# A planner's transfer allowance, due times and slot table changed in a fused attention and gated-MLP kernel

## The chip, the cores and the metric

The program runs on one core of a Trainium2 chip. The metric is the device time of one execution in microseconds (us), lower is better; the number compared is the median of several executions. One execution was also profiled, and the rows below come from that one.

## What is computed

Two modules follow each other. The first is attention with heads mixed before and after the softmax; its output, turned to tokens by features, is the input of a gated block of three matrix products:

```python
# batch, n_heads, seq, head_dim = 4, 12, 448, 64
scores = scale * np.matmul(q, k.transpose(0, 1, 3, 2))
scores = np.einsum('bhij,hg->bgij', scores, w_pre)
scores = scores - np.max(scores, axis=-1, keepdims=True)
attn = np.exp(scores)
attn = attn / (np.sum(attn, axis=-1, keepdims=True) + 1e-09)
attn = np.einsum('bhij,hg->bgij', attn, w_post)
out = np.matmul(attn, v)
...
# n_tokens, d_model, d_ff = 1792, 768, 1536; x is out, heads side by side
gate = 1.0 / (1.0 + np.exp(-(x @ w_gate)))
val = x @ w_val
result = gate * val @ w_out
```

The weights arrive as 64-bit numbers and are cut to 32 bits on the chip. Matrix products of the gated block are done in float16, each float32 operand as a high and a low half (three matmuls instead of one), and blocks of two by two are multiplied with seven products instead of eight.

## The kernel before

**Attention** runs in slots, about 90 of them, each for one or two groups of ten query rows. A slot premixes (L216), takes the row maximum (L221, VectorE), the exponential (L228, ScalarE), scales (L240, GpSimd; L246, VectorE), mixes again (L258) and multiplies by v (L285). What else a slot does stands in a table, `plan`, that `at(slot, fn, ...)` fills. Among this is the preparation of the first eight of 36 weight pieces (`early`): four loads of a piece into one of three raw buffers, then `top` (ScalarE, GpSimd, ScalarE), `convert` and `peak_of` (VectorE) and a store of the float32 piece. A piece takes eleven steps, in eleven slots one after the other, and a new piece begins every eight slots from slot 10.

**The gated block** is a list of some 1,300 tasks that `order_tasks` puts in order before anything is issued. It walks through a clock of its own, gives each task a planned duration (`units`) on TensorE ("pe"), VectorE ("dve"), ScalarE ("act"), GpSimd ("pool"), the transfers that SyncE issues ("dma") or those that GpSimd issues ("keep"), and picks on each the open task with the earliest due time `late`. A task whose buffers are not free, or that would make its result too far ahead of `late` (table `AHEAD`), waits; `LEAVE` says how many buffers of a kind must stay free. The result is only an order: on the chip each engine works its list from the front, and a task whose input is missing holds up all that stand behind it on that engine. After a transfer the clock adds a fixed time before the result counts as there: 2.5 us, or 6.0 (`LATE`) in the part beside the attention.

There are six layers n (256 of the 1,536 hidden columns each) and two pairs p of batches. A layer and pair is seven products P1, P2, P6, P5, P7, P4, P3, each in two halves; a half is nine matmuls of 128x448 into one PSUM bank (`gate`, L1050). Between P1 and P6, and between P7 and P4, ScalarE copies the bank to a buffer of kind T (`copy`, L1070), since the next product is added onto it; sums (L1077) and the gate function (L1080, L1083) follow on VectorE and ScalarE, and the hidden values go to DRAM (`keep_h`, L1015). After all layers come the 21 steps of the output product for p = 0 and then for p = 1 (`out_mm`, L1061), each of three calls of six matmuls.

Every operand of a product is made by `round` (ScalarE, L1029: the high half) and `rest` (VectorE, L1034: the low half), after sums of blocks (`tt`, L1043). Both need a scale, and the scale needs the largest magnitude over all partitions. That is found by a chain: `peak` on VectorE (L924) reduces to one number per partition; `put_peak` (GpSimd, L927) stores 0.5 or 1 KB to DRAM; `get_peak` (SyncE, L930) loads it back spread over all partitions; `weigh` on VectorE (L934, then L910 to L913) gives the scale. The chain runs for layers 2 to 5 (`max_w`), once for w_out (`max_out`) and once for the hidden values of each pair (`max_h`). For w_out there are twelve pieces: raw load, conversion, store (`keep_w`, L999), load (`load_w`, L1002), 21 operands, their store (`keep_pair`, L1037) and, for each p, their load (`load_pair`, L1040). Stores of w_out's operands and the loads back are the transfers `w<-m` and `m<-w`.

## Time and profile before

| | us |
|---|---|
| median of three runs | 852.2 |
| the three runs | 855.54, 846.03, 852.2 |
| the profiled execution | 845.48 |
| its span, first to last instruction | 843.7 |

The profiled execution is 0.8% under the median of the three runs, and 1.78 us of it lie outside the span. Attention fills the first 362 us of the span, the layers stand up to 681 us, the output product for p = 0 up to about 768 and for p = 1 up to 840.

### The profile page before, as it was taken

What the parts mean: (1) busy time and instruction counts of PE and PEld (TensorE: products, weight loads), DVE (VectorE), ACT (ScalarE), POOL (GpSimd) and SP (SyncE); (2) the same over time, 40 slices, a digit from 0 to 9 for tenths busy, and PEclk for the clock granted to TensorE, in tenths of its full rate; (3) what the DMA queues carried; (4) which work ended last, traced back from release to release, by engine and by line L of the source; (5) the groups of instructions that cost most, each with busy time, mean ns of one, the idle gap of its engine ahead of it and who ended that gap; (6) DMA issues with size and microseconds to landing.
All of it is one profiled execution on the core that took longest, in us unless ns stands there. A gap on an engine that the chain in (4) does not pass through costs nothing.

```text
span 843.7 us, 23152 instructions
## 1 busy us (share of the span) xinstructions
PE 776.3 (92%) x9530; PEld 421.7 (50%) x9530; DVE 649.7 (77%) x1069; ACT 551.0 (65%) x1042; POOL 242.4 (29%) x422
## 2 busy tenths in 40 slices
PE   8899998999899998899799999999993997979998
PEld 2455554555455555554355455545551453535554
DVE  4998898889998997899887865799663898556500
ACT  3888887688688886886767655678653764253300
POOL 1544454344444443401122112222230222110000
PEclk9999999999999999999899999999996999989999
DMA  5786678857975756964244215557794798993001
GB/s 196 224 230 190 207 237 253 175 175 225 249 244 173 231 198 151 256 194 156 82 171 160 87 37 189 163 178 271 268 314 111 271 353 337 273 377 137 33 29 70
DMA packets 78689, 166.13 MB, mean 197 GB/s; under 512 B 20984, under 2 KB 54104, under 8 KB 78584
## 3 DMA queue, kind: packets, MB, share of 16 engines
q1 hardware_dynamic: 70920, 136.03, 52.7%
q0 software_dynamic: 7088, 28.13, 8.6%
q8 instruction: 74, 1.21, 0.6%
q10 hardware_dynamic: 576, 0.51, 0.2%
q14 instruction: 31, 0.25, 0.1%
HBM read 87.77 MB, written 38.15 MB: 149 GB/s over the span
## 4 chain that ended last, share of the span: by engine, by line
PE 49%; DMA 14%; DVE 11%; issue 11%; ACT 10%; POOL 3%; SPq 1%; ACTq 0%; POOLq 0%; DVEq 0%
PE bank L1050 17%; PE bank L1061 11%; PE av L285 6%; PE pm L216 5%; PE mx L258 5%; PE qk L158 4%; ACT e L228 4%; DVE m L1034 3%; DMA raws<-in_w_dram 3%; ACT mix L266 2%; DMA T<-st 2%; DVE nm L221 2%; DMA m<-xs 2%; DVE m L1043 1%; DMA m<-max_w 1%
## 5 line engine op out<-in xcount | busy, mean ns | idle before, releaser
L1050 PE MATMUL bank<-m,m 128*128 128x448 f16 x1116 | 217.1, 356 | 23.1 <-ACT m L1070 22.6
L1050 PEld LDWEIGHTS <-m 128*128 128x128 f16 x1512 | 148.6, 98 | 165.9 <-issue 30.4
L228 ACT ACTIVATE e<-pm,nm 128x448 f32<-128x448 f32 x180 | 115.1, 640 | 55.3 <-DVE nm L221 51.5
L240 POOL TENSOR_SCALAR ph<-e,ss 128x448 f16<-128x448 f32 x180 | 112.6, 638 | 62.1 <-DVE ss L234 41.1
L221 DVE TENSOR_REDUCE nm<-pm 128x1 f32<-128x448 f32 x180 | 103.3, 614 | 24.8 <-PE pm L216 23.8
L246 DVE SCALAR_TENSOR_TENSOR pl<-e,ss,ph 128x448 f16<-128x448 f32 x180 | 118.0, 695 | 0.8 <-POOL ph L240 0.8
L1061 PEld LDWEIGHTS <-m 128*128 128x128 f16 x756 | 75.0, 99 | 83.5 <-issue 16.8
L258 PEld LDWEIGHTS <-ph 64*128 64x128 f16 x2880 | 68.3, 94 | 79.0 <-issue 42.7
L266 ACT ACTIVATE mix<-mx 128x960 f32<-128x960 f32 (+1 forms) x92 | 102.8, 1117 | 2.7 <-PE mx L258 2.6
L216 PE MATMUL pm<-T,w 64*64 64x448 f32 (+1 forms) x720 | 99.1, 572 | 2.7 <-DMA T<-st 1.9
L158 PE MATMUL qk<-k,q 64*64 64x448 f32 (+2 forms) x640 | 94.4, 549 | 4.4 <-ACT st L164 4.0
L1061 PE MATMUL bank<-m,m 128*128 128x448 f16 x486 | 96.0, 352 | 0.0
L285 PE MATMUL av<-mix,v 128*64 128x120 f32 (+1 forms) x1504 | 94.0, 269 | 0.9 <-ACT xt L293 0.8
L258 PE MATMUL mx<-w2hi,ph 64*128 64x60 f16 x1440 | 71.9, 189 | 15.2 <-ACT mix L266 14.1
L285 PEld LDWEIGHTS av<-mix,v 128*64 128x64 f32 x1504 | 74.5, 139 | 8.2 <-issue 2.9
L1050 PE MATMUL bank<-m 128*128 128x448 f16 x396 | 77.4, 352 | 1.3 <-DVE m L1077 1.1
L233 POOL TENSOR_SCALAR ss<-ss 128x2 f32<-128x2 f32 (+1 forms) x92 | 35.6, 387 | 136.8 <-ACT e L228 136.0
L258 PE MATMUL mx<-w2lo,ph 64*128 64x60 f16 x1440 | 71.3, 188 | 3.0 <-issue 3.0
L258 PE MATMUL mx<-w2hi,pl 64*128 64x60 f16 x1440 | 71.2, 188 | 0.6 <-DVE pl L246 0.5
L258 PEld LDWEIGHTS <-pl 64*128 64x128 f16 x1440 | 62.0, 94 | 0.8 <-DVE pl L246 0.6
L1077 DVE TENSOR_TENSOR m<-bank,m 128x448 f32<-128x448 f32 x72 | 44.3, 618 | 22.3 <-ACT m L1070 10.8
L987 POOL CAST raws<-raws 128x768 f16<-128x768 bf16 x36 | 33.9, 943 | 93.8 <-ACT raws L984 93.8
(115 smaller groups left out, 1032.0 us busy)
## 6 DMA issues: line engine op xcount, KB each, us to landing
T<-st SPq DMA_DIRECT2D x176, 210.0 KB
m<-w SPq DMA_DIRECT2D x62, 384.0 KB
raws<-in_w_dram SPq DMA_DIRECT2D x28, 767.6 KB
hs<-m POOLq DMA_DIRECT2D x48, 224.0 KB, 2.6
m<-hs SPq DMA_DIRECT2D x15, 672.0 KB
w<-m POOLq DMA_DIRECT2D x21, 384.0 KB, 5.4
v<-in_vb_dram SPq DMA_DIRECT2D x12, 512.0 KB
raws<-in_w_dram SPq DMA_DIRECT2D x32, 191.9 KB
```

Source lines behind the costliest of these rows:

```text
L158: nc.tensor.matmul(sc[e][s0:s1, :S], lhsT=q[rows, c, s0:s1], rhs=k[rows, :], start=True, stop=True)
L216: nc.tensor.matmul(pm[bank][64 * x:64 * x + 64, :S], lhsT=w1[rows], rhs=T[rows, x], start=True, stop=True)
L221: nc.vector.tensor_reduce(nm[:, i:i + 1], pm[bank][:, :S], axis=AX.X, op=ALU.max, negate=True)
L228: nc.scalar.activation(out=e_t[u][:, i], in_=pm[units[u][2][i]][:, :S], func=AF.Exp, bias=nm_t[u][:, i:i + 1], scale=1.0, accum_out=ss_t[u ...
L240: nc.gpsimd.tensor_scalar(ph[:, i], e_t[u][:, i], ss_t[u][:, i:i + 1], 1.0, op0=ALU.mult, op1=ALU.mult)
L246: nc.vector.scalar_tensor_tensor(pl[:, i], e_t[u][:, i], ss_t[u][:, i:i + 1], p_t[u][0][:, i], op0=ALU.mult, op1=ALU.subtract)
L258: nc.tensor.matmul(mx[:, x, i, jb * HK:(jb + 1) * HK], lhsT=p[rows, i, JB[jb]:JB[jb] + 128], rhs=w[rows], start=(k == 0), stop=(k == 2))
L266: nc.scalar.activation(out=out.rearrange("p g (y r) -> p y g r", r=HALF), in_=mx_t.pop(u), func=AF.Copy, scale=1.0 / (P_UP * W_UP))
L285: nc.tensor.matmul(av_t[bi][64 * i:64 * i + 64, c % 4, :n], lhsT=vt[b, u][:, h + i, jb, :], rhs=mixes[bi % 2][:, jb, 2 * c + i, :n], start ...
L1050: self.nc.tensor.matmul(self.f32(bank), lhsT=w[a][:, k], rhs=x[b][:, k], start=self.START[i] and k == r == 0, stop=k == self.KH - 1 and r ...
L1061: self.nc.tensor.matmul(self.f32(bank), lhsT=w[a][:, k], rhs=b[bb], start=self.START[i] and j == k == r == 0, stop=j == OUT_TILES - 1 and ...
L1077: self.nc.vector.tensor_tensor(self.f32(out), self.f32(bank), self.f32(snap), op=ALU.add)
```

## The change

Seven things change. The names `w`, `wp`, `wq`, `q`, `T` are kinds of buffer or operand.

- Every planned transfer counts as landed 6.0 us after it (it was 2.5 in the gated block). The planned durations of a few tasks grow too.
- A table `DUE` moves the due times of groups of tasks: a group's tasks count as due so many us earlier (numbers below zero do nothing), and w_out's raw pieces and operands get due times of their own, from 120 and 127 us on the planner's clock.
- `AHEAD` and `LEAVE` get other numbers; the last region has seven buffers of kind T instead of five, and w_out's pieces may lie in buffers of kind B.
- The order of the first products: layer 1's P1 and P2 stand before layer 0's P6.
- The steps of an early raw piece stand in slots 0, 1, 2, 3 (the loads), then 8 to 12 and 14, a new piece begins every seven slots from slot 6.
- Small tiles that held top, up and down scales become parts of one tile.
- `sum_of` loops over the parts of its sum; there is one part, as before.

```diff
     for k in range(moe.EARLY):
-        for step in range(11):
-            at(10 + 8 * k + step, moe.early, k, step)
+        for step, slot in enumerate((0, 1, 2, 3, 0, 8, 9, 10, 11, 12, 14)):
+            at(6 + 7 * k + slot, moe.early, k, step)
         if k % 4 == 3:
-            for step in range(4):
-                at(20 + 8 * k + (0, 1, 3, 5)[step], moe.early_bound, k // 4, step)
+            for step, slot in enumerate((14, 15, 18, 21)):
+                at(6 + 7 * k + slot, moe.early_bound, k // 4, step)
...
-    LEAVE = dict(w=6, wp=1, wq=1, q=3, qp=1)
+    LEAVE = {'w': 7, 'wp': 3, 'wq': 12, 'q': 1, 'qp': 0}
...
-    ROOM = ((-15, dict(B=9, A=8)), (-7, dict(B=2, A=2, T=3)), (0, dict(B=3, A=5)), (9.6, dict(B=5, A=8, T=5, R=0)))
-    AHEAD = dict(raw=250.0, half=250.0, w=50.0, s=12.0, t=15.0, wp=15.0, wq=25.0, q=40.0, qp=15.0,
-                 c=40.0, snap=40.0, tmp=40.0, wide=40.0, hq=60.0, hqp=50.0, ow=120.0, os=120.0, owp=120.0)
+    DUE = {('raw', 2): -12.8, ('bound', 'w', 2): 72.0, ('w', 2): 20.3, ('raw', 3): -44.5, ('bound', 'w', 3): 106.5,
+        ('w', 3): -65.8, ('raw', 4): -107.6, ('bound', 'w', 4): 109.6, ('w', 4): -93.5, ('raw', 5): -334.4,
+        ('bound', 'w', 5): -183.5, ('w', 5): -156.2, ('w', 1): -149.8, ('x', 1): -35.5, ('bound', 'h', 0): -295.4,
+        ('h', 0): -462.6, ('bound', 'h', 1): 179.3, ('h', 1): -27.5, ('load_h', 0): 9.6, ('load_pair', 0): -8.7,
+        ('store', 0): -57.0, ('keep_h', 0): -7.8, ('sum_of', 0): 125.4, ('sigmoid', 0): 22.8, ('hidden', 0): -7.6,
+        ('copy', 0): -5.8, ('sum', 0): 54.2, ('load_x', 0): -59.0, 'raws': (120.6, 11.4), 'pairs': (127.3, 180.1)}
+    ROOM = ((-15, dict(B=9, A=8)), (-7, dict(B=2, A=2, T=3)), (0, dict(B=3, A=5)), (9.6, dict(B=5, A=8, T=7, R=0)))
...
+        steps = [(n, p, i) for n, p in order for i in range(NP)]
+        for at in (2, 3):
+            steps.insert(at, steps.pop(NP + at - 2))
+        for n, p, i in steps:
...
-            us = min(t.units.values()) + (2.5 if "dma" in t.units or "keep" in t.units else 0.1)
+            us = min(t.units.values()) + (self.LATE if "dma" in t.units or "keep" in t.units else 0.1)
...
+        for t in tasks:
+            t.late = min(t.late, self.soon(t))
...
-                end = now + us + ((2.5 if now >= 0 else self.LATE) if u in ("dma", "keep") else 0.1)
+                end = now + us + (self.LATE if u in ("dma", "keep") else 0.1)
...
+    def soon(self, t):
+
+        group = self.group(t)
+        if group[0] in ("raws", "pairs"):
+            first, step = self.DUE[group[0]]
+            lead = {self.load_raw: 15.0, self.top: 6.0, self.keep_w: -3.0, self.load_w: 15.0}.get(t.fn, 0.0)
+            return first + step * group[1] - lead
+        return t.late - self.DUE.get(group, 0.0)
```

Three places show what this does to the order. The first is **ScalarE in the layer stage p = 1, n = 4**, around the first work that needs the scale of p = 0's hidden values. Rows with `up_h0` (before) are operands that need this scale, rows with `one_out0` (after) need w_out's; COPY rows are the copies of a bank that free it for the next product. Before:

```order
L1070 COPY m_3_8615<-bank0_8447 128x448
L921 ACTIVATE junk_201,abs_h1_175<-m_3_8615 128x448
L1070 COPY m_3_8615<-bank1_8448 128x448
L1029 ACTIVATE m_0_7946<-m_3_8615,up_h0_167 128x1344
L1029 ACTIVATE m_2_8510<-m_2_8510,up_h0_167 128x1344
L1029 ACTIVATE m_3_8615<-m_0_7946,up_h0_167 128x1344
L1070 COPY m_1_8294<-bank0_8447 128x448
L1070 COPY m_1_8294<-bank1_8448 128x448
```

and the same place after the change:

```order
L1126 COPY m_1_8259<-bank0_8416 128x448
L1126 COPY m_3_8578<-bank1_8417 128x448
L1136 ACTIVATE m_3_8578<-m_3_8578,back1_166 128x448
L1085 ACTIVATE m_0_7912<-m_0_7912,one_out0_160 128x768
L1085 ACTIVATE m_3_8578<-m_2_8476,one_out0_160 128x768
L1085 ACTIVATE m_3_8578<-m_0_7912,one_out0_160 128x768
L976 ACTIVATE junk_167,abs_h1_159<-m_3_8578 128x448
L1126 COPY m_1_8259<-bank0_8416 128x448
L1126 COPY m_3_8578<-bank1_8417 128x448
```

Three operands of w_out stand there now, where three of the hidden values stood; the first operand with h0's scale comes 24 rows later.

The second place is **VectorE at the end of the layer stage p = 0, n = 5 and the beginning of the next**, between w_out's `peak` and its `weigh` (the reduction into top_out0, or one_out0, from an m tile). The L1077 rows (after: L1133) are sums of a bank of TensorE. Before:

```order
L924 TENSOR_REDUCE top_out0_176<-abs_out0_180 128x1
L1043 TENSOR_TENSOR m_1_8294<-m_1_8294,m_0_7946 128x1344
L1034 SCALAR_TENSOR_TENSOR m_0_7946<-m_3_8615,up_h0_167,m_0_7946 128x1344
L1034 SCALAR_TENSOR_TENSOR m_2_8510<-m_2_8510,up_h0_167 128x1344
L1077 TENSOR_TENSOR m_3_8615<-bank2_8449,m_1_8294 128x448
L1077 TENSOR_TENSOR m_3_8615<-bank3_8450,m_1_8294 128x448
L1034 SCALAR_TENSOR_TENSOR m_3_8615<-m_0_7946,up_h0_167,m_3_8615 128x1344
L934 TENSOR_REDUCE top_out0_176<-m_1_8294 128x1
```

and after:

```order
L980 TENSOR_REDUCE one_out0_160<-abs_out0_162 128x1
L1133 TENSOR_TENSOR m_3_8578<-bank6_8583,m_1_8259 128x448
L1133 TENSOR_TENSOR m_3_8578<-bank7_8584,m_3_8578 128x448
L1139 SCALAR_TENSOR_TENSOR m_3_8578<-m_3_8578,back0_165 128x448
L1139 SCALAR_TENSOR_TENSOR m_3_8578<-bank5_8582,back0_165,m_3_8578 128x448
L1133 TENSOR_TENSOR m_3_8578<-bank6_8583,m_1_8259 128x448
L1133 TENSOR_TENSOR m_1_8259<-bank7_8584,m_3_8578 128x448
L1139 SCALAR_TENSOR_TENSOR m_3_8578<-m_1_8259,back0_165,m_3_8578 128x448
L980 TENSOR_REDUCE one_h0_154<-abs_h0_156 128x1
L1133 TENSOR_TENSOR m_3_8578<-bank2_8418,m_1_8259 128x448
L990 TENSOR_REDUCE one_out0_160<-m_3_8578 128x1
```

w_out's chain now begins first, and h0's `peak` stands inside it. Between the two ends of w_out's chain the sums run from P7 on bank 6 over P3 on banks 6 and 7 to the next stage's P2 on bank 2, eight halves of products; before they ran over two sums of one product.

The third place is **SyncE's list in the output product of p = 0**, around the load of the second pair's largest hidden value. L1040 (after: L1096) loads an operand of w_out, L1019 (L1075) a block of hidden values. Before:

```order
L1040 DMA m_2_8510<-w16_132 128x1536
L1019 DMA m_3_8615<-hs_133 128x1344
L1019 DMA raws_63<-hs_133 128x1344
L1040 DMA m_3_8615<-w16_132 128x1536 x3
L930 DMA m_3_8615<-max_h1_174 128x128
L1040 DMA m_2_8510<-w16_132 128x1536
```

and after:

```order
L1096 DMA m_0_7912<-w16_132 128x1536
L1096 DMA m_3_8578<-w16_132 128x1536
L1096 DMA m_2_8476<-w16_132 128x1536
L986 DMA m_3_8578<-max_h1_158 128x128
L1075 DMA m_2_8476<-hs_133 128x1344
L1096 DMA m_0_7912<-w16_132 128x1536 x3
```

The load of max_h1 stood behind 21 of the 42 loads of w_out's operands and behind all blocks of hidden values; now it stands behind 8 of them and ahead of the second pair's blocks.

## Rows read from the trace of the kernel before

**Rows 1.** The page, part 1: busy us, share of the span, instructions.

```profile
PE 776.3 (92%) x9530; PEld 421.7 (50%) x9530; DVE 649.7 (77%) x1069; ACT 551.0 (65%) x1042; POOL 242.4 (29%) x422
```

**Rows 2.** TensorE's timeline: start, us, line, count, [idle before <- who ended it].

```profile
406.32 10.08 PE L1050 MATMUL bank<-m,m 128*128 128x448 f16 x45 [7.06 <-ACT m L1070]
...
485.91 44.43 PE L1050 MATMUL bank<-m,m 128*128 128x448 f16 x234
...
648.23 8.59 PE L1050 MATMUL bank<-m,m 128*128 128x448 f16 x36 [14.67 <-ACT m L1070]
656.66 6.97 PE L1050 MATMUL bank<-m 128*128 128x448 f16 x36
...
713.61 4.93 PE L1061 MATMUL bank<-m 128*128 128x448 f16 x18 [4.92 <-DMA m<-w]
...
745.23 6.17 PE L1061 MATMUL bank<-m 128*128 128x448 f16 x18 [6.26 <-ACT m L1068]
```

**Rows 3.** ScalarE's timeline around 612 to 662 us.

```profile
643.74 4.03 ACT L1029 ACTIVATE m<-m,up_h 128x1344 f16<-128x1344 f32 x3 [13.08 <-DVE up_h L913]
647.67 0.94 ACT L1070 COPY m<-bank 128x448 f32<-128x448 f32 x2
```

**Rows 4.** VectorE's timeline, same stretch.

```profile
622.47 0.17 DVE L924 TENSOR_REDUCE top_h<-abs_h 128x1 f32<-128x24 f32 x1
...
642.66 0.29 DVE L934 TENSOR_REDUCE top_h<-m 128x1 f32<-128x128 f32 x1 [11.42 <-DMA m<-max_h]
...
643.62 0.15 DVE L924 TENSOR_REDUCE top_out<-abs_out 128x1 f32<-128x12 f32 x1
...
656.74 0.29 DVE L934 TENSOR_REDUCE top_out<-m 128x1 f32<-128x128 f32 x1 [5.81 <-DMA m<-max_out]
```

**Rows 5.** VectorE's and ScalarE's timelines around 715 to 750 us.

```profile
727.00 0.17 DVE L924 TENSOR_REDUCE top_h<-abs_h 128x1 f32<-128x24 f32 x1
...
742.16 0.29 DVE L934 TENSOR_REDUCE top_h<-m 128x1 f32<-128x128 f32 x1 [10.53 <-DMA m<-max_h]
...
743.25 1.42 ACT L1029 ACTIVATE m<-m,up_h 128x1344 f16<-128x1344 f32 x1 [18.56 <-DVE up_h L913]
```

**Rows 6.** VectorE's timeline around 430 to 450 us.

```profile
435.29 0.15 DVE L924 TENSOR_REDUCE top_w<-abs_w 128x2 f32<-128x8 f32 x1
...
444.91 0.42 DVE L934 TENSOR_REDUCE top_w<-m 128x2 f32<-128x256 f32 x1 [2.59 <-DMA m<-max_w]
```

**Rows 7.** Tile view of max_h, then of max_w: time to landing of the stores.

```profile
DMA to landing us min/median/max: 8.0/10.7/13.4
...
DMA to landing us min/median/max: 3.2/3.2/3.7
```

**Rows 8.** Busy time by stretch: TensorE, its weight loads, VectorE, ScalarE, GpSimd, clock, DMA.

```profile
380.00:400.00 20.00, 19.21 (x101) 9.76 (x100) 20.00 (x28) 14.19 (x24) 3.34 (x2) 1.00 0.42 158
500.00:520.00 20.00, 20.00 (x108) 10.32 (x107) 10.92 (x14) 10.23 (x20) 3.27 (x5) 1.00 0.46 156
660.00:680.00 20.00, 19.53 (x104) 9.90 (x102) 20.00 (x25) 17.05 (x29) 5.40 (x10) 1.00 0.93 315
```

**Rows 9.** Transfers by line: count, KB each, median us to landing.

```profile
w<-m POOLq DMA_DIRECT2D x21, 384.0 KB, 5.4
```

**Rows 10.** What SyncE waited for, 600 to 745 us: total, times, longest.

```profile
SPq L1040 <- DMA w<-m: 62.7, 19, 10.2
```

**Rows 11.** Waits in the attention, 30 to 360 us: ScalarE, then TensorE.

```profile
ACT raws L984 <- DMA raws<-in_w_dram: 5.1, 2, 2.8
...
PE pm L216 <- DMA T<-st: 1.9, 3, 0.9
```

**Rows 12.** The chain that ended last, its transfers of 40 to 260 us.

```profile
62.67 5.10 DMA raws<-in_w_dram
...
128.90 7.20 DMA raws<-in_w_dram
...
220.96 8.22 DMA T<-st
```

More of the change, by code (lines that the diff above doesn't have):

```diff
@@ L512, in __init__ @@
         for g, (e, c) in list(groups.items()) + [(("x", p), (1, 0)) for p in pairs]:
-            for kind in ("top", "up", "down"):
-                self.one[(kind,) + g] = top.tile([128, e], F32, name="%s_%s%d" % ((kind,) + g))
+            one = top.tile([128, 3 * e], F32, name="one_%s%d" % g)
+            for i, kind in enumerate(("top", "up", "down")):
+                self.one[(kind,) + g] = one[:, i * e:(i + 1) * e]
             if c:
@@ L518, in __init__ @@
         for p in pairs:
+            back = top.tile([128, 2 * self.FN + 1], F32, name=f"back{p}")
             for n in range(self.FN + 1):
-                self.one["back", p, n] = top.tile([128, 2 if n < self.FN else 1], F32, name=f"back{p}_{n}")
+                self.one["back", p, n] = back[:, 2 * n:min(2 * n + 2, 2 * self.FN + 1)]
         self.junk = top.tile([128, 512], F16, name="junk")
@@ L583, in split @@
         uses = ((by, False),) if known else ()
-        more = 0.15 if by[1] == "w" else 0.0
+        more = 0.25 if by[1] == "w" else 0.07
         self.task(self.round, dict(act=self.by_act(n)["act"] + more), ((f, False), (pair, True)) + uses, pair, f, by)
@@ L745, in gathered @@
         if i in (P1, P6, P7):
-            task(self.copy, self.by_act(S), [(a, False), (("snap", p, n, i, e), True)] + more, ("snap", p, n, i, e), a, back)
+            task(self.copy, dict(act=0.53 if n < self.FN else 0.63), [(a, False), (("snap", p, n, i, e), True)] + more, ("snap", p, n, i, e), a, back)
         if i in (P2, P7, P3):
@@ L816, in order_tasks @@
                     need = self.place(t, free)
-                    if t.late + lag - now > 40.0 and any(free.get(self.KIND[name[0]], 0) < dict(raw=2).get(name[0], 0)
+                    if t.late + lag - now > 40.0 and any(free.get(self.kind(name), 0) < dict(raw=2).get(name[0], 0)
                                                          for name in t.new if name[0] in self.KIND):
@@ L855, in order_tasks, with group, tile_of, kind @@
                 self.users[name] = self.users.get(name, 0) + 1
+    def soon(self, t):
[5 more added lines that the diff above has]
+        return t.late - self.DUE.get(group, 0.0)
+    def group(self, t):
+        N, a = 4 * self.FN, t.args
+        if t.fn in (self.load_raw, self.top, self.convert, self.keep_w, self.peak_of):
+            k = a[{self.load_raw: 0, self.top: 0, self.peak_of: 2}.get(t.fn, 1)]
+            if t.fn == self.peak_of:
+                k += N if a[1][0] == "out" else 4 * a[1][1]
+            return ("raws", k - N) if k >= N else ("raw", k // 4)
+        if t.fn in (self.peak, self.put_peak, self.get_peak, self.weigh):
+            return ("raws", 4 * OUT_TILES) if a[0][0] == "out" else ("bound",) + a[0]
+        if t.fn in (self.load_w, self.round, self.rest, self.tt, self.keep_pair):
+            name = a[1] if t.fn in (self.round, self.rest) else a[0]
+            if t.fn == self.keep_pair:
+                return "pairs", a[1]
+            if name[0] in ("w", "s", "wp"):
+                n = self.order[name[2]][0] if name[0] == "w" else name[2]
+                return ("pairs", n - self.FN) if n >= self.FN else ("w", n)
+            return ("h", name[1][0]) if type(name[1]) is tuple else ("x", name[1])
+        return t.fn.__name__, 0
+    def tile_of(self, name):
+        if name[0] == "w" and name[2] >= 4 * self.FN:
+            return self.order[name[2]][0] - self.FN
+        if name[0] in ("s", "wp") and name[2] >= self.FN:
+            return name[2] - self.FN
+        return -1
+    def kind(self, name):
+        return "B" if name[0] in ("w", "s") and self.tile_of(name) >= 0 else self.KIND.get(name[0])
     def ahead(self, name):
@@ L896, in f32 @@
             return self.banks[name[1]][:, :self.S]
-        return self.at[name][:, :self.WE] if name[0] == "raw" else self.at[name]
+        return self.at[name][:, :self.WE] if name[0] in ("raw", "w", "s") else self.at[name]
     def f16(self, name):
@@ L920, in sum_of @@
     def sum_of(self, h, g, c):
[L921 removed]
+        h, e = self.f32(h), self.abs[g].shape[2]
+        n = h.shape[1] // e
+        for i in range(e):
+            self.nc.scalar.activation(out=self.junk[:, :n], in_=h[:, i * n:(i + 1) * n], func=AF.Abs,
+                                      accum_out=self.abs[g][:, c, i:i + 1])
     def peak(self, g):
```

48 lines of the change are left out of this document (24 added, 24 removed).

## The prediction, made before the changed kernel was run

> **What bounds the kernel now.** The page's first part says that TensorE is busy for 776.3 of the 843.7 us of the span [rows 1]; so only its idle time can be won, and the next view is TensorE's timeline after the attention, read for the brackets that give idle time and who ended it. Four idle times stand out [rows 2]. The chain of waits, followed back from each, names the cause.
>
> A: 14.67 us before 648.23. It ended with ScalarE's copy of a bank, which stood behind three operands that needed h0's scale; those had waited 13.08 us [rows 3]. The scale was late since the chain peak, store, load, weigh took from 622.47 to 642.66, 20.2 us; VectorE had reached `weigh` 11.42 us before the answer came [rows 4].
> B: 7.06 us before 406.32, between layer 0 and layer 1, again on a copy [rows 2].
> C: 4.92 us before 713.61, on a load of an operand of w_out (m<-w) in p = 0's output product [rows 2].
> D: 6.26 us before 745.23. h1's chain took from 727.00 to 742.16, 15.2 us; VectorE waited 10.53 of them, ScalarE 18.56 [rows 2, 5].
>
> After an idle time TensorE starts slowly. After A 36 matmuls took 8.59 us where the next 36 took 6.97: 1.6 more. 234 in a row took 44.43, so 0.190 each; by that 45 are 8.55 and 18 are 3.42 us, and the restarts after B, C and D cost 1.5, 1.5 and 2.75 [rows 2]. So A is worth 16.3, B 8.6, C 6.4 and D 9.0 us, 40.3 in all. Nearly all else after the attention is matmuls that must be done.
>
> **A and the longer allowance.** The planner let 2.5 us pass after each transfer; a chain of store and load was thus planned far too short. In the task list before, four to six halves of products stand between `peak` and `weigh` of every chain; after the change eight for w_out, nine for h0, eight or nine for layers 2 to 5, and fourteen calls for h1. A half is nine matmuls, 1.71 us; a call of the output product six, 1.14 us. That gives w_out's chain 13.7 us of covered time, h0's 15.4 and h1's 16.0. Measured lengths of the chain are 9.6 us for a layer [rows 6], 13.1 for w_out's (643.62 to 656.74), 20.2 for h0's [rows 4] and 15.2 for h1's [rows 5]. By its own length w_out's wait is nil and h0's 4.8; by the shortest nil, by the longest 6.5 for w_out. An idle us of VectorE cost TensorE 14.67 / 11.42 = 1.3. h0's length was taken while GpSimd's small store queued among w_out's raw pieces; in SyncE's new list eleven transfers stand between the last of these and h0's load (it was three). I therefore take 2 of A's 16.3 us as left: gain 14.3, bounds 16.3 and 7.9 (6.5 x 1.3 left). What hides the longer wait is the sums and the operands of the earlier products that VectorE and ScalarE do meanwhile; in the place of h0's three operands before the two copies stand three of w_out's, which hang on the other chain. If that is late, the same copies are late again.
>
> One rule speaks against the six us. The row says that the landing of a store of half a KB took 8.0 to 13.4 us for h and 3.2 to 3.7 for the layers [rows 7]. The Trainium skill, page "DMA: Bandwidth & Descriptors", section "Anatomy of one DMA — SWDGE (gpsimd) path", gives such a store a fixed 2.0 us or so and size over bandwidth on top; by it 2.5 us would do, A and D would owe nothing to the allowance, and the sum below would hold 12.0 in place of 34.8 us. The trace disagrees, by 1.2 us in calm stretches and by 11 in full ones.
>
> **D, by the due time of h1's bound.** It moves from behind 21 loads of operands to behind 8. Covered time 16.0 us against its own 15.2: nothing is left; against 20.2, 4.2 x 1.3 = 5.5. I take 0.5 left: gain 8.5, bounds 9.0 and 3.5. Late next there is VectorE itself: it is busy for all of 20 us at 660 to 680 [rows 8].
>
> **C, operands of w_out.** The load that was missing is that of the ninth step (P6, last third). Before, its operand's store stands eight calls ahead of its use (9.1 us) and the load five; the trace made this 9.1 + 4.92 = 14.0 us. Now fourteen calls lie between store and use, 16.0 us, so it fits by 2. In SyncE's list the load is eleventh among its kind, not fourteenth, but h1's load now stands ahead of it, and behind SyncE's wait for h1's store are queued all loads of operands and blocks: at the longest landing of 13.4 us [rows 7] that is 7.4 more than planned. The store of an operand lands in 5.4 us as a median [rows 9], and SyncE waited 62.7 us for these in 19 waits, 10.2 the longest [rows 10]; 10.2 would make 14.0 into 18.8, 2.8 us of idle time and a slow start. Bounds: 6.4 gained, or 0.5 lost (7.4 less the 2 that fit is 5.4, and the start's 1.5, against 6.4 now). I take 5.
>
> **B, the swapped products and more T buffers.** Layer 1's P1 and P2, four halves or 6.8 us, now stand ahead of layer 0's P6, on inputs that layer 0's P1 and P2 have already used; two more T buffers let the copies go. That covers most of B, if the operands are there. Against it: at 380 to 400 VectorE is busy for 20.00 of 20 us [rows 8], so that it, not the order, may set the pace, and layer 1's operands must now be made before others. Bounds 8.6 gained, 3.4 (one product) lost; I take a little under half of what B is worth, 4.
>
> **w_out's pieces, the layers' chains.** Twelve raw loads, conversions and stores move to earlier layers, beside TensorE work that hides them; five of w_out's raw pieces now stand ahead of the layers' last eight. That costs nothing while the chains of layers 3 and 5 have fourteen halves from `peak` to first use, 23.9 us, against 9.6 [rows 6] or at worst 20.2 [rows 4]. Tiles joined, the loop in `sum_of`, the longer planned durations: no instruction is added, nothing.
>
> **Attention.** ScalarE waited 5.1 us in two waits for raw pieces [rows 11], and the chain that ended last goes through raw loads of 5.10 and 7.20 us [rows 12]. Five slots instead of two between the last load and its use remove these. But a piece every seven slots puts loads at other slots, in front of other loads of T, and one of these of 8.22 us is on the chain too [rows 12]. Bounds 5.1 gained, 8.2 lost; since TensorE waited for T for 1.9 us in all [rows 11], I take 3 gained.
>
> **Sum.** 14.3 + 8.5 + 5 + 4 + 3 = 34.8 us. The span goes from 843.7 to 808.9; with 1.8 us outside it the profiled execution from 845.5 to 810.7. The median stands at 852.2 / 845.48 = 1.008 times the profiled one, so 817. A measurement of this kernel can tell a difference from none from about 1% on.
>
> **Rivals.**
> Traffic decides. A landing is not a constant: it grows with what is under way, 3.2 to 13.4 us in one trace [rows 7], and six us only fits the calm stretches. Every chain beside the output product then takes h0's 20.2 us: A gains 7.9, D 3.5, C 2.1 (2.8 and a 1.5 restart stay), B 4, the attention nothing: 17.5, a profiled execution of 828, a median of 835. The Trainium skill has the rule in the same page, section "Queues, rings and completion order": a semaphore's increment lands only after every earlier write of its DMA engine, across its queues. The three lengths of one chain agree with it. Against it speaks that w_out's raw pieces are out of the way.
>
> VectorE becomes the bound. At 660 to 680 it has no gap [rows 8]; if what C and D lose in waits returns as operands that come just too late, A, B and the attention remain, 21.3: 824, a median of 831. Against it: in the middle of the layers it is busy for only 10.92 of 20 us [rows 8], and the earlier pieces go there.
>
> It doesn't do what it says. The list does show the wider chains; but if the idle time only moves (to layers 3 and 5, whose `weigh` now stands six halves before the first use instead of about twenty), within 1% of now: 848.
>
> Slower: the early raw pieces block the regrouping of the scores. SyncE's list is worked from the front, eight pieces bring 32 loads into other slots, and each T behind them holds up a slot. If each piece costs one T wait of 8.22 us where three raw waits cost about 17.5 on the chain now (two of them in [rows 12], the third about as long as the first), that is 65.8 - 17.5 = 48 us in the attention against 31.8 won after it: 862 profiled, a median of 869. It decides from (31.8 + 8.5 + 17.5) / 8, some 7 us per piece on. Against it: the 1.9 us that TensorE waited for T [rows 11].
>
> **How the numbers follow.** The forecast with its own scatter (806 to 826) has 0.56, traffic 0.18, VectorE 0.12, no change 0.07, slower 0.07. The likeliest is the forecast: 817. All gains at their best (16.3 + 9.0 + 6.4 + 8.6 + 5.1 = 45.4) give 807 as a median, and the runs before lie 0.7% below theirs: low end 804. The high end takes in most of the traffic rival: 838. Faster by over 1% (under 843.7) are the forecast, traffic and VectorE: 0.86; the same 0.08; slower 0.06.
>
> **What would show it.** In the profile after: the three `weigh` rows of h0, w_out and h1 with little idle time before them; no TensorE idle time over 3 us in the layers' second half; SyncE's load of h1 soon after the output product begins; ScalarE without waits for raw pieces in the attention. Wrong would be: idle before `weigh` as long as now, an m<-w wait on TensorE again, slots of the attention over 6 us more often than now, or VectorE busy without a gap while TensorE waits.

## The result

The changed kernel takes 822.6 us (median of four executions, 821.23 to 825.83) against 852.2 (846.03 to 855.54): a ratio of 0.9666, 95% interval 0.9603 to 0.9729. The forecast was 817, with a range of 804 to 838.

The profiled executions differ by less, 845.48 to 825.83, since the one of before is 6.7 us under its median and the one of after 3.2 above: 19.7 + 6.7 + 3.2 = 29.6. So the stages below add up to the smaller difference. In the spans (843.7 and 824.1) the three stages moved thus: the first `gate` product begins at 362.63 before and 370.85 after, 8.2 us lost; from there to the first product of w_out 318.7 and 305.4, 13.3 won; the output product 162.4 and 147.9, 14.5 won.

The page of the changed kernel, part 1, answers to [rows 1]; TensorE has the same number of matmuls.

```profile
PE 773.0 (94%) x9530; PEld 420.4 (51%) x9530; DVE 650.3 (79%) x1069; ACT 554.0 (67%) x1042; POOL 243.6 (30%) x422
```

TensorE's timeline after the change answers to [rows 2]. L1106 is `gate`, L1117 `out_mm`, L1085 and L1090 make operands, L1133 is a sum of two banks.

```profile
384.64 0.55 PE L1106 MATMUL bank<-m,m 128*128 128x448 f16 x2 [2.91 <-ACT m L1085]
...
386.64 13.67 PE L1106 MATMUL bank<-m,m 128*128 128x448 f16 x62 [1.45 <-DVE m L1090]
...
638.06 3.52 PE L1106 MATMUL bank<-m,m 128*128 128x448 f16 x9 [6.19 <-DVE m L1133]
641.38 3.99 PE L1106 MATMUL bank<-m 128*128 128x448 f16 x18
...
704.41 7.55 PE L1117 MATMUL bank<-m,m 128*128 128x448 f16 x39 [0.78 <-DMA m<-w]
```

The bracket of D (6.26) is gone, C is 0.78 for 4.92, B 2.91 and 1.45 for 7.06. B still has a slow start: 62 matmuls at 0.190 are 11.8 us and took 13.67, so 6.3 of B's 8.6 us remain. A is still there with 6.19 and a slow start: 9 matmuls at 0.190 are 1.71 and 18 are 3.42 us, so 3.52 and 3.99 hold another 2.4. Of A's 16.3 us 8.6 remain.

Who holds A is seen in VectorE's timeline, the answer to [rows 4, 5]: `peak` (L980) and `weigh` (L990) of w_out, of h0, of h1.

```profile
611.13 0.17 DVE L980 TENSOR_REDUCE one_out<-abs_out 128x1 f32<-128x12 f32 x1
...
622.14 0.18 DVE L980 TENSOR_REDUCE one_h<-abs_h 128x1 f32<-128x24 f32 x1 [0.74 <-ACT junk L976]
...
636.39 0.29 DVE L990 TENSOR_REDUCE one_out<-m 128x1 f32<-128x128 f32 x1 [10.60 <-DMA m<-max_out]
...
646.56 0.28 DVE L990 TENSOR_REDUCE one_h<-m 128x1 f32<-128x128 f32 x1
...
680.44 0.17 DVE L980 TENSOR_REDUCE one_h<-abs_h 128x1 f32<-128x24 f32 x1
...
699.13 0.29 DVE L990 TENSOR_REDUCE one_h<-m 128x1 f32<-128x128 f32 x1 [2.33 <-DMA m<-max_h]
```

It is w_out's chain now: 25.3 us from `peak` to `weigh`, where it was 13.1, and VectorE waits 10.60 us for it. Both of its transfers are long. The store goes out at 611.59, the load can follow at 624.94, and its data are there at 636.39 (timelines of GpSimd and of SyncE's queue):

```profile
611.59 0.54 POOL L983 DMA_DIRECT2D max_out<-one_out  x1 [0.35 <-DVE one_out L980]
...
624.94 0.32 SPq L986 DMA_DIRECT2D m<-max_out  x1
```

h0's chain takes 24.4 and h1's 18.7, but with nine halves and fourteen calls ahead of their `weigh` VectorE waits for h0's not at all and for h1's 2.33 us. ScalarE's operand behind w_out's scale waits 10.98, and the sum that TensorE waits for at 638 stands behind `weigh` on VectorE. The tile views of max_h, max_out and max_w, for [rows 7], say how long the stores of the peaks took to land:

```profile
DMA to landing us min/median/max: 11.8/12.6/13.5
...
DMA to landing us min/median/max: 13.3/13.3/13.3
...
DMA to landing us min/median/max: 3.5/4.7/6.3
```

So the layers' stores of 1 KB landed after 4.7 us as a median, and the half KB of h's and w_out's, near the output product, after 11.8 to 13.5. The busy time by stretch, for [rows 8], shows that VectorE is not what holds A: at 620 to 640 it works for 5.47 of 20 us. At 380 to 400, where B was, it still has no gap.

```profile
380.00:400.00 20.00, 15.50 (x74) 7.15 (x72) 20.00 (x26) 13.86 (x23) 0.00 (x0) 0.91 0.80 269
...
620.00:640.00 20.00, 13.81 (x69) 6.86 (x68) 5.47 (x13) 4.81 (x9) 1.62 (x3) 0.88 0.77 144
...
660.00:680.00 20.00, 20.00 (x107) 10.33 (x106) 18.75 (x23) 17.61 (x27) 4.02 (x8) 1.00 0.85 301
```

In the attention, TensorE's waits and the chain that ended last (the first of its loads; all are counted from 0 to 365 us) answer to [rows 11, 12]. ScalarE no longer waits for raw pieces, as forecast; but loads of T are on the chain seven times with 50.7 us, where it was three times with 18.3, and TensorE's own wait for T is 4.7 for 1.9.

```profile
PE pm L216 <- DMA T<-st: 4.7, 6, 2.4
```

```profile
106.81 2.79 DMA T<-st
...
133.75 8.59 DMA T<-st
...
153.62 10.88 DMA T<-st
...
165.95 5.09 DMA raws<-in_w_dram
...
191.53 8.55 DMA T<-st
```

Three questions follow. What of the 28 us after the attention comes from the six us, and what from the order? Did the new slots cost the 8.2 us in the attention? Why do the chains take 24 us, and can A's rest be had?

### The profile page after: what moved, and what is told of

Its sections match the earlier page's. It is cut to its first block, busy times and chain, and to the rows that moved or that the text cites. A ratio compares the mean times of both kernels' runs of the same rounds, so it can differ in the third digit from the quotient of the medians.

```text
span 824.1 us, 23147 instructions
## 1 busy us (share of the span) xinstructions
PE 773.0 (94%) x9530; PEld 420.4 (51%) x9530; DVE 650.3 (79%) x1069; ACT 554.0 (67%) x1042; POOL 243.6 (30%) x422
## 4 chain that ended last, share of the span: by engine, by line
PE 61%; DMA 14%; ACT 10%; DVE 9%; issue 5%; POOL 1%; SPq 0%; ACTq 0%; DVEq 0%; POOLq 0%
PE bank L1106 27%; PE bank L1117 14%; DMA T<-st 6%; PE av L285 6%; PE pm L216 6%; PE mx L258 4%; PE qk L158 4%; ACT e L228 4%; DVE nm L221 3%; ACT mix L266 2%; DVE m L1090 2%; DMA max_out<-one_out 2%; DMA m<-max_out 1%; ACT st L164 1%; DVE pl L246 1%
## 5 line engine op out<-in xcount | busy, mean ns | idle before, releaser
L1106 PE MATMUL bank<-m,m 128*128 128x448 f16 x1116 | 217.7, 356 | 11.0 <-DVE m L1133 6.2
L1106 PEld LDWEIGHTS <-m 128*128 128x128 f16 x1512 | 148.5, 98 | 152.7 <-issue 11.4
L1117 PEld LDWEIGHTS <-m 128*128 128x128 f16 x756 | 73.9, 98 | 70.1 <-DMA m<-w 1.2
L216 PE MATMUL pm<-T,w 64*64 64x448 f32 (+1 forms) x720 | 102.3, 570 | 5.4 <-DMA T<-st 4.7
L1117 PE MATMUL bank<-m,m 128*128 128x448 f16 x468 | 93.1, 352 | 0.8 <-DMA m<-w 0.8
L285 PEld LDWEIGHTS av<-mix,v 128*64 128x64 f32 x1504 | 73.0, 136 | 14.1 <-issue 8.0
L1106 PE MATMUL bank<-m 128*128 128x448 f16 x396 | 78.3, 354 | 0.0
L1043 POOL CAST raws<-raws 128x768 f16<-128x768 bf16 x36 | 39.0, 1082 | 120.7 <-ACT raws L1040 120.7
L233 POOL TENSOR_SCALAR ss<-ss 128x2 f32<-128x2 f32 (+1 forms) x92 | 31.0, 337 | 143.0 <-ACT e L228 141.8
L1133 DVE TENSOR_TENSOR m<-bank,m 128x448 f32<-128x448 f32 x72 | 44.6, 621 | 24.4 <-PE bank L1106 16.7
```

Source lines behind the costliest of these rows:

```text
L216: nc.tensor.matmul(pm[bank][64 * x:64 * x + 64, :S], lhsT=w1[rows], rhs=T[rows, x], start=True, stop=True)
L285: nc.tensor.matmul(av_t[bi][64 * i:64 * i + 64, c % 4, :n], lhsT=vt[b, u][:, h + i, jb, :], rhs=mixes[bi % 2][:, jb, 2 * c + i, :n], start ...
L1106: self.nc.tensor.matmul(self.f32(bank), lhsT=w[a][:, k], rhs=x[b][:, k], start=self.START[i] and k == r == 0, stop=k == self.KH - 1 and r ...
L1117: self.nc.tensor.matmul(self.f32(bank), lhsT=w[a][:, k], rhs=b[bb], start=self.START[i] and j == k == r == 0, stop=j == OUT_TILES - 1 and ...
L1133: self.nc.vector.tensor_tensor(self.f32(out), self.f32(bank), self.f32(snap), op=ALU.add)
```

## Experiments

"After" is the changed kernel, "before" the old one; every ratio is to runs of before on the same chip. After itself stands at 0.9666.

**The slots of the early raw pieces, put back and alone.**

```diff
-        for step, slot in enumerate((0, 1, 2, 3, 0, 8, 9, 10, 11, 12, 14)):
-            at(6 + 7 * k + slot, moe.early, k, step)
+        for step in range(11):
+            at(10 + 8 * k + step, moe.early, k, step)
...
-            for step, slot in enumerate((14, 15, 18, 21)):
-                at(6 + 7 * k + slot, moe.early_bound, k // 4, step)
+            for step in range(4):
+                at(20 + 8 * k + (0, 1, 3, 5)[step], moe.early_bound, k // 4, step)
```

> The changed kernel, with the early raw pieces of the attention back in the slots of before (10 + 8k + step). In the profile after the change the first gate stands 8.2 us later than before (370.85 against 362.63), though the prediction gave the slots 3 us of gain. Theory, the slots cost: the new slots put loads ahead of more loads of T; with the old ones the first gate comes back to 361 to 365 and the median falls by 6 to 9 us, from 822.6 to about 815. Rival, scatter of single executions: the profiled executions before and after are the fastest and the slowest of their four, and the first gate stays within 3 us of 367 for either set of slots; median 820 to 825. Second rival, the predicted term was right and the profile misleads: ScalarE's two waits for raw pieces come back and the median rises by 3, to 826.

The mirror image, the new slots in the kernel before:

> The kernel before with nothing but the new slots of the early raw pieces: the same question with the other ten edits left out. Slots cost: first gate at 368 to 373, median 858 to 861 where before has 852. Scatter: within 3 us of before. Predicted gain: 849.

Measured: old slots in after 818.95 (0.961, 0.9565 to 0.9655); new slots in before 857.28 (1.0061, 1.003 to 1.0092). By the ratios the new slots cost 4.8 and 5.2 us, less than the 6 to 9 expected, the first with overlapping intervals, the second clear of one. The first gate of the profile with the old slots in after, an execution of 823.87, the longest of its six, stands at 367.3, which the rival of scatter allows too. What decides is the second ratio and the first gates of all profiles: with the old slots 362.6 to 367.3 us in four kernels (mean 364.5), with the new 367.5 to 376.4 in ten (mean 370.9). ScalarE's waits for raw pieces are back with the old slots in after (5.8 us), and its attention is shorter all the same. The loads of T on the chain show where the time goes: with the new slots in the old kernel six, 38.1 us in sum:

```profile
107.49 2.80 DMA T<-st
...
134.16 10.04 DMA T<-st
...
155.54 9.33 DMA T<-st
...
191.55 9.02 DMA T<-st
```

These stand at the same places as in after, and in the three other kernels with old slots that chain holds two, two and one load of T (11.8, 10.4 and 7.7 us). Over all profiles the sum of these loads is 7.7 to 18.3 us with the old slots and 21.2 to 50.7 with the new. These sums do not measure the loss (the latest first gate, 376.4, goes with 22.4 us); they tell the two sets of slots apart. The theory that the slots cost holds; scatter alone and the predicted gain fall.

**The six us, taken away and alone.**

```diff
-                end = now + us + (self.LATE if u in ("dma", "keep") else 0.1)
+                end = now + us + ((2.5 if now >= 0 else self.LATE) if u in ("dma", "keep") else 0.1)
```

and the same 2.5 in the pass from the end, in after; the reverse in before.

> The changed kernel with 2.5 us in place of six after each planned transfer beyond the attention; due times, swapped products, early operands of w_out and slots stay. In its list four or five halves of products stand between peak and weigh of a layer's, w_out's and h0's chain instead of eight or nine, and six calls instead of fourteen in h1's. Theory, the six us are what wins at A and D: 4 halves cover 6.8 us of w_out's and h0's chains of about 25 us where 8 and 9 covered 13.7 and 15.4, and six calls cover 6.8 of h1's 18.7; so A's left-over of 8.4 us grows by 7 to 9, D's idle time of 6 to 9 us comes back, the layers' copies wait again: +13 to +18, a median of 836 to 841. Rival, the order wins (due times and room for w_out's operands), and a late weigh only shifts the same wait: within 5 us of 822.6.

> The kernel before with nothing but six us in place of 2.5 after each planned transfer. Its list has eight or nine halves between peak and weigh instead of four to six, twelve calls in h1's chain instead of six; w_out's pieces and operands stay where they were. Theory, the six us alone win at A and D: A's 16.3 us shrink to 8 or less, D's 9.0 to 5 or less, B and C stay: 838 to 842. Rival, the wait needs the due times and the room: later operands put the idle time elsewhere (C grows), 848 or more.

Measured: 840.67 (0.9898, 0.9856 to 0.994) without the six us, 837.67 (0.9861, 0.9831 to 0.9891) with them alone. Both agree with the theory, the second 0.3 us below its range. In the first, VectorE's and TensorE's timelines show A back, and part of D:

```profile
621.34 0.29 DVE L990 TENSOR_REDUCE one_out<-m 128x1 f32<-128x128 f32 x1 [14.84 <-DMA m<-max_out]
```

```profile
625.48 9.07 PE L1106 MATMUL bank<-m,m 128*128 128x448 f16 x36 [10.88 <-ACT m L1126]
...
742.77 5.05 PE L1117 MATMUL bank<-m,m 128*128 128x448 f16 x18 [3.54 <-ACT m L1124]
```

In the second A shrinks to 1.27, and a part of the rival is there too: an operand of w_out comes 13.34 us too late for the first output product:

```profile
632.76 5.27 PE L1050 MATMUL bank<-m,m 128*128 128x448 f16 x27 [1.27 <-ACT m L1070]
...
676.11 6.35 PE L1061 MATMUL bank<-m 128*128 128x448 f16 x18 [13.34 <-DMA m<-w]
```

So the six us win 1.4% alone, all else wins 1.0% without them, and together they win 3.3%.

**The due times, left out, and those of w_out alone.**

```diff
-            t.late = min(t.late, self.soon(t))
+            t.late = min(t.late, t.late)
```

> The changed kernel without its due times; six us, swapped products, w_out's room in the B buffers and the slots stay. In its list w_out's peak stands after call 162 instead of 136 and six halves before its weigh, h1's after call 194 instead of 173. Theory, due times give what the six us alone don't: the kernel before with six us alone took 13 of the 28 us, and its output product began with 13.34 us of waiting for an operand of w_out. Without due times that wait is back, 8 to 13 us: a median of 831 to 836. Rival, the rest comes from the swapped products and the T buffers (between the layers): the output product begins without a wait, 820 to 826.

```diff
-            t.late = min(t.late, self.soon(t))
+            t.late = min(t.late, self.soon(t) if self.group(t)[0] in ("raws", "pairs") else t.late)
```

> The changed kernel with the due times of w_out's pieces and operands alone; those of the layers' pieces, of h0's and h1's chains, of the copies and sums are left out. Without any due time the kernel took 848.6, with 25.9 us of waits for an operand of w_out in the output product. In this list w_out's peak stands after call 137 (after the change 136, without due times 162), h1's after call 203 (173, 194). Theory, w_out's early operands are nearly the whole worth of the due times: no wait for an operand of w_out over 2 us, D's idle time of 4 to 6 us is back since h1's chain is late, a median of 823 to 830. Rival, the layers' and h1's due times hold half of it: 832 or more.

Measured: 848.64 without any (0.9989, 0.9958 to 1.0021), no faster than before; 826.17 with those of w_out alone (0.9728, 0.9683 to 0.9773). Without due times TensorE's timeline has no bracket over 3.2 us left in the layers, and two in the output product:

```profile
683.53 5.00 PE L1117 MATMUL bank<-m,m 128*128 128x448 f16 x18 [15.27 <-DMA m<-w]
...
716.13 9.16 PE L1117 MATMUL bank<-m,m 128*128 128x448 f16 x36 [10.58 <-DMA m<-w]
```

That is 25.9 us where 8 to 13 were expected, and the median is 26.0 above after's. The two do not match one to one: the brackets in the layers shrank, so the listed idle time from the first gate on is 19.6 us longer than after's, and the profiled execution 21.2. The other parts of the change make this wait longer than six us alone do; which of them was not tried. With w_out's due times alone no idle time is listed in the output product, and the ratio's interval overlaps that of after, so what the other due times are worth can't be told from nothing. That also refutes the part of the expectation on D: h1's `peak` stands at 710.92 there, 30 us later than in after, and its `weigh` still waits for only 0.41 us, so D does not need a due time for h1.

```profile
727.40 0.29 DVE L990 TENSOR_REDUCE one_h<-m 128x1 f32<-128x128 f32 x1 [0.41 <-DMA m<-max_h]
```

**Layer 1's products in their old place.**

```diff
-        for at in (2, 3):
-            steps.insert(at, steps.pop(NP + at - 2))
```

> The changed kernel with layer 1's P1 and P2 behind layer 0's P6 again. Theory, the swap is what shortened the wait between layers 0 and 1: idle time there goes from 4.4 us (2.91 and 1.45) back to about 7, median up by 2 to 4, to 825 to 827. Rival, the T buffers or VectorE's pace set it (VectorE was busy for 20.00 of 20 us there): the same within 2 us, 821 to 825. Second rival, the swap costs, since operands of layer 1 are wanted sooner: a gain of 2 to 4.

Measured: 820.56 (0.9696, 0.9656 to 0.9736): no difference from after that the runs can tell. The brackets at 384 and 386 are gone, and one of 2.50 stands 110 us later (L1104 is `gate` here, L1083 makes an operand):

```profile
496.42 12.06 PE L1104 MATMUL bank<-m,m 128*128 128x448 f16 x54 [2.50 <-ACT m L1083]
```

The last experiment, also without the swap, shows the same: no bracket over 0.4 us up to 400, and 2.50 at 491. All nine kernels with the changed tables and the swap have 3.2 to 6.4 us of brackets between 379 and 395. So without the swap B's 7.06 us are gone entirely: what takes them away is another part of the change, and the swap puts a wait there. Six us alone leave 4.82 of them; the further T buffers, `AHEAD` and `LEAVE` were not tried alone.

**The stores of the peaks on another queue.**

```diff
-        (eng or self.nc.gpsimd).dma_start(out=self.maxima[g], in_=self.one[("top",) + g])
+        (eng or self.nc.scalar).dma_start(out=self.maxima[g], in_=self.one[("top",) + g])
```

> The changed kernel with the stores of the peaks issued from ScalarE's queue; these stores alone, half a KB or one KB each. In the trace after the change w_out's peak landed 13.3 us after its issue at 611.59; GpSimd had issued two stores of an operand of w_out and three of hidden values in the 5.7 us ahead of it. Theory, GpSimd's own queue makes the landing long: the store no longer stands behind these, lands in 3 to 6 us, VectorE's wait of 10.60 us before w_out's weigh falls under 4 and TensorE's 6.19 us at 638 goes, median down by 5 to 8, to 815 to 818. Rival, the traffic of all queues makes it long: landings stay at 10 to 14 us and the median within 3 us of 822.6, or above it if ScalarE now waits for VectorE's peak with its copies behind it.

Measured: 826.39 (0.9752, 0.971 to 0.9795), not faster than after. The landing is not recorded for this queue, but SyncE's load of the peak, which waits for the store, tells it: SyncE stood waiting for w_out's store (9.2 us) and for both of max_h (14.1 for the longer), so the load goes out when the store has landed. The timelines of ScalarE's queue and of SyncE's:

```profile
617.22 0.33 ACTq L983 DMA_DIRECT2D max_out<-one_out  x1
...
633.78 0.33 ACTq L983 DMA_DIRECT2D max_h<-one_h  x1
```

```profile
632.03 0.32 SPq L986 DMA_DIRECT2D m<-max_out  x1
...
648.72 0.32 SPq L986 DMA_DIRECT2D m<-max_h  x1
```

From store to load it is 14.8 and 14.9 us, and 12.0 for h1's; with GpSimd's queue it was 13.3 for w_out's (611.59 to 624.94). GpSimd's queue is not the cause. VectorE's wait before w_out's `weigh` did fall to 3.96, as the theory had it, but not by the store: w_out's chain is 3.6 us shorter (616.87 to 638.58) since the load behind the store took 6.5 us where it was 11.4. VectorE waits 5.60 before h0's `weigh` instead, and A's one bracket of 6.19 has become five of 0.93 to 3.17, 7.8 in sum. The first gate of this profile, the longest of the six executions, stands at 376.4, 5.5 us later: the peaks of the layers that are made in the attention kept SyncE's queue, so why was not found.

**More traffic at the layers' peaks.**

```diff
     def put_peak(self, g, eng=None):
+        if g[0] == "w" and eng is None:
+            for k in range(3):
+                self.nc.scalar.dma_start(out=self.dump[g, k].bitcast(I8)[:, :8 * self.WE - 3], in_=self.src[k].bitcast(I8)[:, 3:])
```

> The changed kernel with traffic added where the layers' chains run: three copies of 768 KB from memory to memory, from ScalarE's queue, just ahead of each of the four stores of max_w on GpSimd's queue. Nothing reads the copies. Theory, the landing of a small store grows with what is under way on any queue: the four landings go from 3.5 to 6.3 us (median 4.7) to 9 to 14, VectorE waits before the layers' weigh, which it does not now, and the median rises by 4 to 10. Rival, it is the queue of its own or the kind of chain (w against h and out) that sets it: landings stay at 3.5 to 7 and the median within 3 us of 822.6.

Measured: 840.49 (0.989, 0.9844 to 0.9936). The tile view of max_w, and two rows of VectorE's and TensorE's timelines:

```profile
DMA to landing us min/median/max: 7.7/10.0/10.2
```

```profile
464.17 0.42 DVE L994 TENSOR_REDUCE one_w<-m 128x2 f32<-128x256 f32 x1 [3.35 <-DMA m<-max_w]
```

```profile
497.40 5.25 PE L1110 MATMUL bank<-m 128*128 128x448 f16 x18 [2.74 <-ACT m L1130]
```

The landing doubled, from 4.7 to 10.0 (3.2 to 5.2 as the median in every other profile that records it), though the copies went through another queue than the stores: what is under way on other queues lengthens it. That w_out's and h's stores are long for the same reason is likely, but by analogy, since no run took traffic away from them. Nor does traffic at the moment explain all: w_out's store of before landed after 7.3 us, while the DMA engines were busy for 0.03 of that time (max_out's tile view, then the stretch; the last two numbers are the DMA share and GB/s):

```profile
DMA to landing us min/median/max: 7.3/7.3/7.3
...
644.10:651.40 7.30, 3.17 (x9) 1.31 (x9) 6.83 (x6) 6.38 (x7) 0.50 (x1) 0.50 0.03 10
```

The loss of 18 us is more than the 4 to 10 expected. VectorE's waits before `weigh` are 4.7 us in all, and the idle time listed for TensorE in the layers is 20.6 us for 10.8; how much of that comes from other transfers that the copies delay was not separated. (L994 is `weigh` here, L1110 `gate`, L1130 a copy.)

**More than six us: 12 for the peaks alone, eight for everything.**

```diff
-                end = now + us + (self.LATE if u in ("dma", "keep") else 0.1)
+                end = now + us + (12.0 if t.fn in (self.put_peak, self.get_peak) and now >= 0 else self.LATE if u in ("dma", "keep") else 0.1)
```

and the same 12 in the pass from the end.

> The changed kernel with an allowance of 12 us in place of six for the store and the load of the peaks alone; all other transfers keep six. Between peak and weigh stand 14 to 17 halves for the layers, 16 for w_out, 19 for h0, 18 calls for h1. Theory, the length of the chains (24 to 25 us) against the planned wait is what is left at A: 16 halves are 27 us, so VectorE's 10.60 us before w_out's weigh and TensorE's 6.19 at 638 go, with the slow start 8.4 us: a median of 814 to 817. Rival, the later weigh leaves too little time for the operands of h0 and of w_out: the idle time moves to the last halves before the output product or into it, and the median stays at 822 or rises to 830.

```diff
-    LATE = 6.0
+    LATE = 8.0
```

> The changed kernel with eight us in place of six after every planned transfer. With 2.5 the median was 840.7, with six 822.6, with 12 for the peaks alone 831.5. Between peak and weigh stand 12 halves for w_out's and 11 for h0's chain instead of eight and nine. Theory, there is an optimum: each longer wait makes the operands behind it later, so that eight wins A's 6 us and gives back as much in small waits; 819 to 827. Rival, six is still too short for the chains of 24 us: 814 to 818. Second rival, already past the optimum as with 12 for the peaks: 828 or more.

Measured: 831.52 (0.9812, 0.9771 to 0.9854) and 837.63 (0.9863, 0.9822 to 0.9905): both slower than after, and six is the best of the values tried. With 12 us for the peaks no `weigh` waits any longer and TensorE works for 20.00 of 20 us at 620 to 640, but the listed idle time from the first gate to the end is 15.4 us where after has 11.6. With eight TensorE's timeline shows operands that come too late:

```profile
604.20 12.88 PE L1106 MATMUL bank<-m,m 128*128 128x448 f16 x54 [4.03 <-ACT m L1085]
...
709.22 0.90 PE L1117 MATMUL bank<-m 128*128 128x448 f16 x2 [3.85 <-DVE m L1090]
```

Its listed idle time is 16.1 us, 4.5 more than after's, where the median is 15 higher and the profiled execution 10.4; 6.8 of these lie in the output product. What makes up the rest was not found.

**The two parts that brought nothing, undone together.**

> The changed kernel with the two parts that brought nothing undone: old slots of the early raw pieces and no swap of layer 1's products. Theory, the slots cost 4 to 5 us (ratios 0.961 against 0.9666, and 1.0061 for the slots alone) and the swap nothing: a ratio to before of 0.958 to 0.964, some 815 to 819, faster than both kernels. Rival, the two don't add up, since an earlier start of the layers meets operands that are late: a ratio of 0.966 or more.

Measured: 815.23 (0.9606, 0.9568 to 0.9645), executions of 811.28 to 818.61 where after has 821.23 to 825.83. It is the fastest kernel by its median. The intervals of the two ratios overlap, and it stands where the old slots alone stand (0.961), so undoing the swap adds nothing. The longest bracket that is left of A hangs on h0's chain, for whose `weigh` VectorE waits 5.92 us:

```profile
641.32 6.95 PE L1104 MATMUL bank<-m,m 128*128 128x448 f16 x27 [3.34 <-DVE m L1131]
```

## Why the prediction came out right, and where its steps did not

The sum was 34.8 us, and the medians differ by 29.6. The mechanism after the attention was right: A, C and D were chains of transfers planned too short and operands of w_out planned too late, and 27.8 of the forecast's 31.8 us came there in the profiled executions. Three terms were mis-sized: the attention, with the wrong sign, and A and B, of which about half came. Short brackets that the prediction left out (2.5 us before, 0.2 after) gave another 2.3.

Part of the agreement is luck. The profiled executions differ by 19.7 us, not 34.8, and 825.83 lies nearer to the traffic rival's 828 than to the forecast's 810.7; the other 9.9 us between the medians are the scatter of these two executions. One profile speaks for the medians: that of the kernel before with the new slots, an execution at its median (857.16, median 857.28). Its first gate stands at 370.77, after's at 370.85, and it takes 31.4 us more from there on than after does. That is 3.6 more than the profile of before shows, so about half of the 6.7 us by which that one is under its median seems to lie behind the first gate.

**Attention: +3 forecast, about -5 measured.** The failed step is "I take 3 gained". The first half of it held: ScalarE's 5.1 us of waits for raw pieces are gone. The second half was the bound of 8.2 us on loads of T behind loads of raw pieces; it was dismissed because TensorE waited for T for only 1.9 us. That wait was the wrong row. TensorE's wait stayed small (4.7), while the chain, which goes through these loads, took 32 us more of them and 12 us less of raw pieces. The slower rival named this mechanism, with one wait of 8.22 us for each piece and 48 us lost in all; the eight pieces cost about 5 together.

**A: 14.3 forecast, 7.7 measured.** The failed step is "By its own length w_out's wait is nil". The length, 13.1 us, became 25.3 at its new place, 13.3 for the store and 11.4 for the load, against 13.7 us of covered time; the bound of 7.9 in the traffic rival was the right value. What is left of A varies: with the same eight and nine halves of cover the brackets between 600 and 665 us sum to 6.4 in after, 6.0 with the old slots, 5.1 and 2.8 in the two kernels without the swap. The prediction had put the long chain of before down to GpSimd's queue ("while GpSimd's small store queued among w_out's raw pieces"). On ScalarE's queue the store is as long, and added traffic on another queue makes a short one long. What the Trainium skill, page "DMA: Bandwidth & Descriptors", section "Queues, rings and completion order", says of a semaphore's increment, that it lands after every earlier write of its DMA engine, across its queues, agrees with both runs, which do not single this mechanism out. The fixed 2.0 us or so that the Trainium skill gives on the same page, section "Anatomy of one DMA — SWDGE (gpsimd) path", does not agree: no small store of GpSimd's queue landed in under 3 us, and those near the output product took 7.3 to 13.5 in the profiles before and after. An allowance of 2.5 us cost 18 us.

**D: 8.5 forecast, 9.0 measured,** but by another step than "by the due time of h1's bound". With w_out's due times alone D is nil as well, with thirteen calls of cover instead of fourteen.

**C: 5 forecast; 4.1 of idle time and the slow start after it went.** The size was right and what hangs on it was not seen: TensorE waits 13.34 us for w_out's operands with six us alone and 25.9 with all of the change but the due times, and w_out's due times are enough to prevent this. A term was missing in the prediction: what the longer allowance would have cost without them.

**B: 4 forecast, 2.3 measured.** Idle time went from 7.06 to 4.36, and the slow start stayed. The failed step is that the swapped products cover "most of B": without the swap this wait is gone, another of 2.50 stands later, and the time is the same. VectorE still has no gap at 380 to 400, which the prediction gave as the reason against; that it sets the pace there is argued, no run tried it.

**The layers' chains: 0 forecast,** and rightly: no layer's `weigh` waits.

Of the signs named, h1's early load and ScalarE without waits for raw pieces came true. Two failed: VectorE waits 10.60 us before w_out's `weigh`, where it was 5.81, and A's 6.19 are an idle time over 3 us in the layers' second half. The traffic rival, with 17.5 us, was right on A alone among its terms. VectorE did not become the bound. Two slips in the prediction change nothing: the low end of 804 does not follow from 807 less 0.7%, which is 801, and the layers' stores in [rows 7] are of 1 KB, not half a KB.

## What to carry to other kernels

A planner's allowance for a transfer is a price with two sides. Too short, the engine that needs the answer stands idle with its queue behind it (2.5 us cost 18); too long, everything that takes the covered place comes late (8 cost 15), and raising it pays in full only together with due times for what it pushes back (six us alone 0.9861; all of the change but the due times 0.9989; with w_out's due times 0.9728; all of it 0.9666). When a transfer is moved in an attention of slots, look at the chain that ended last for the transfers that it will stand ahead of, not at what TensorE waits for.

## What the runs showed of the hardware

On GpSimd's queue the changed kernel's stores of 1 KB landed after 3.5 to 6.3 us beside the layers' traffic, and those of half a KB after 11.8 to 13.5 near the output product; on ScalarE's queue the latter took 12.0 to 14.9. Three copies of 768 KB on a different queue raised the layers' median from 4.7 to 10.0. One half KB took 7.3 us with hardly any other transfer under way. TensorE stood idle for 6.19 us up to 638.06; its granted clock was 0.50 from 638 to 642, which is the 1.2 of its two levels of 1.2 and 2.4 GHz, and 0.97 as a mean over the 4 us after that:

```profile
638.00:642.00 4.00, 3.94 (x11) 1.57 (x11) 3.90 (x6) 3.91 (x8) 1.63 (x3) 0.50 0.61 199
642.00:646.00 4.00, 3.78 (x20) 1.84 (x19) 4.00 (x5) 3.97 (x6) 1.61 (x3) 0.97 0.60 241
```
